# The last piece of w_down in fifteen loads of unequal rows

## The chip, the cores and the metric

The kernel runs on one core of one Trainium2 chip. The metric is the device time of one execution in microseconds. All numbers here are in float32, and all data come from HBM through one stream that the host has laid out in the order in which the kernel loads it.

## The reference

One decode step of two parallel branches, added to the input:

```python
B, Sq, D = 2, 1, 512;  Hq, Hkv, Sk, Dh = 32, 32, 8192, 128;  F = 1376
W = 2048                                   # the last 2048 cached positions
xn = layernorm(x)
q = (xn @ wq).reshape(B, Sq, Hq, Dh).transpose(0, 2, 1, 3)
scores = einsum("bhqd,bhkd->bhqk", q, k_cache[:, :, Sk - W:]) * Dh ** -0.5
o = einsum("bhqk,bhkd->bhqd", softmax(scores), v_cache[:, :, Sk - W:])
attention = o.transpose(0, 2, 1, 3).reshape(B, Sq, Hq * Dh) @ wo
ffn = ((xn @ w_gate) * (xn @ w_up)) @ w_down
return x + attention + ffn
```

Nearly all bytes are the two caches: 32 heads of 128 x 4096 numbers each, for keys and for values, where the 128 partitions hold 64 slices of the positions for each of the two batch entries.

## The kernel before

`loads()` is a hand-written list of loads in the order of their issue. Each entry is a step number, a buffer and the fields that the load brings: `k` and `v` are one head of a cache (4096 columns), `wq` a piece of the query projection, `wo` one head's 512 columns of the output projection, `wd` 128 rows of w_down (512 columns), `wg` and `wu` the gate weights. Three buffers of 13824 columns (`step0` to `step2`) are used in turn, and a small one (`extra`) holds the first fields and one late head of values.

`build()` first walks over the list, lays the fields side by side in their buffer and puts one load for each entry into `queue`: all 128 partitions, the columns of its fields, and the next stretch of the stream. `issue(upto)` then sends the queued loads up to a step to the queue of the engine SP. The last call, `issue(99)`, sends the loads of step 24: the values of head 31, then w_down pieces 1 to 4, 5 to 7, and 8 and 9. They go into buffer 0, over columns whose earlier contents have been used.

For each head of keys VectorE (DVE) multiplies the tile by the query and sums over the 128 numbers of a position (`products`, `sums`); for each group of four heads it forms the softmax weights (`weights`, with ScalarE's exponentials), and TensorE (PE) multiplies the weights with the values (`weigh`), gathers the parts (`fold`, `gather`, `scaled`) and applies the output projection (`wo`). PE also runs the feed-forward branch; `down(c, ...)` multiplies its hidden vector with w_down piece `c`. There are `NFC` = 10 such full pieces, numbered 0 to 9, and a rest of 96 rows that ScalarE's queue loads at the start (`wr`).

Most results add up in the PSUM bank `acc`. The last few go to another bank, `acc_g`, as `[128, 128]` blocks (`add_groups`: four matmuls for each piece). The end of `build()` is written out by hand:

```python
for i in range(5, 8):
    down(i, add_rows, (i - 5), last=True)
dve.tensor_tensor(acc_sb, acc, xr, op=ALU.add)
wo(d, add_groups)
for i in range(8, NFC):
    down(i, add_groups)
add_groups(id4, acc_sb, last=True)
dve.tensor_copy(o_out, acc_g)
pr.load("SP", out, o_out)
```

So `acc_sb`, on DVE, takes the sums of everything up to piece 7; PE meanwhile multiplies the last head, piece 8 and piece 9, then adds `acc_sb` by a matmul with a small selection matrix, DVE copies the block out of PSUM and SP stores it.

`Program` records every operation and works out the dependencies from the boxes that each one reads and writes. In `emit()` each load gets a semaphore of its own that is complete at 16; an operation that depends on several others gets a separate wait instruction for each but the last (line 196), which is attached to the operation itself (line 197). All operations are emitted from line 197, so groups are told apart here by their tiles.

Of the kernel before, what the change touches and what calls it, by code (L numbers as in the profile page):

```python
# [10 lines left out]
P = 128  # L11
# [8 lines left out]
NFC = F // P  # L20
# [8 lines left out]
CK, CO = J * DH, D  # L29
# [6 lines left out]
def loads():  # L36


    def units(kind, *ids):
        w = {"k": CK, "v": CK, "wo": CO, "wd": CO, "wq": HG * DH}[kind]  # L40
        return [(kind, i, w) for i in ids]

    def wq(g, *cs):
        return units("wq", *[(g, c) for c in cs])

    big = {
        1: units("k", 0, 1, 2),
        3: units("k", 3, 4) + units("v", 0),
        4: units("k", 5, 6) + units("v", 1),
        5: units("k", 7, 8) + units("v", 2),  # L50
    }
    k, v = 9, 3
    for n in range(6, 20):
        i = 1 + n % 2
        big[n] = units("k", *range(k, k + i)) + units("v", *range(v, v + 3 - i))
        k, v = k + i, v + 3 - i
    big[20] = units("k", 30, 31) + units("v", 24)
    big[21] = units("v", 25, 26, 27)
    big[22] = units("v", 28, 29)
    small = {  # L60
        1: wq(1, 0, 1, 2),
        3: wq(1, 3) + wq(2, 0, 1),
        4: wq(2, 2, 3) + units("wd", 0),
        5: wq(3, 0, 1, 2),
        6: units("wo", 0, 1, 2),
        7: wq(3, 3) + units("wo", 3) + wq(4, 0),
        8: units("wo", 4, 5, 6),
        9: units("wo", 7) + wq(4, 1, 2),
        10: wq(4, 3) + wq(5, 0, 1),
        11: units("wo", 8, 9, 10),  # L70
        12: units("wo", 11) + wq(5, 2, 3),
        13: wq(6, 0, 1, 2),
        14: units("wo", 12, 13, 14),
        15: units("wo", 15) + wq(6, 3) + wq(7, 0),
        16: units("wo", 16, 17, 18),
        17: units("wo", 19) + wq(7, 1, 2),
        18: wq(7, 3),
        19: units("wo", 20, 21, 22),
        20: units("wo", 23, 24, 25),
        21: units("wo", 26, 27),  # L80
        22: units("wo", 28, 29, 30, 31),
    }
    out = [
        (0, "x", [("c", 0, CX)] + wq(0, 0, 1, 2, 3)),
        (1, 0, big[1] + small[1]),
        (2, 1, [(w, 0, NC * F) for w in ("wg", "wu")]),
        (3, 2, big[3] + small[3]),
    ]
    for n in range(4, 23):
        out += [(n, (1, 0, 2)[(n - 4) % 3], big[n] + small[n])]  # L90
    out += [
        (23, "x", units("v", 30)),
        (24, 0, units("v", 31)),
        (24, 0, units("wd", 1, 2, 3, 4)),
        (24, 0, units("wd", 5, 6, 7)),
        (24, 0, units("wd", 8, 9)),
    ]
    return out


class Program:
# [133 lines left out]
def build(nc, stream, x_nat, wd_rest, out):  # L235
# [38 lines left out]
    got, used, queue, pos = {}, {}, [], 0  # L274
    for n, t, fields in loads():
        tile = buf_x if t == "x" else buf[t]
        c0 = used.get(n, 0)
        for kind, i, w in fields:
            c = used.get(n, 0)
            got[kind, i] = tile[:, c : c + w]  # L280
            used[n] = c + w
        c1 = used[n]
        assert c1 <= tile.shape[1], (n, c1)
        src = stream[pos : pos + P * (c1 - c0)].rearrange("(p i) -> p i", p=P)
        pos += P * (c1 - c0)
        queue.append((n, tile[:, c0:c1], src))
# [17 lines left out]
    c0 = got["c", 0]  # L304
# [193 lines left out]
    def has(n, kind):  # L498
        return [i for k, i, _ in plan.get(n, []) if k == kind]

    plan = {}
    for n, _, fields in loads():
        plan.setdefault(n, []).extend(fields)
# [19 lines left out]
    for n in range(3, 21):  # L523
        ks, vs = has(n, "k"), has(n, "v")
# [86 lines left out]
def laid_out(x):  # L611

    import numpy as np

    a = x["A_x"].reshape(B, D)
    xs = np.zeros((P, CX), a.dtype)
    xs[:, : B * NC] = a.reshape(B, P, NC).transpose(1, 0, 2).reshape(P, B * NC)
    o = B * NC
    for r in range(4):
        for n in range(N):  # L620
            xs[4 * n + r :: 32, o + r * N + n] = 1.0
    o += 4 * N
    for n in range(HG):
        for q in range(4):
            xs[32 * q + n, o + 4 * n + q] = 1.0
    o += 4 * HG
    for n in range(NFB):
        for b in range(B):
            xs[32 * n + b, o + n * B + b] = 1.0
    o += 2 * NFB  # L630
    for j in range(4):
        for b in range(B):
            xs[32 * j + b, o + b] = 1.0
    xs[:, o + 2 :] = a[:, 0]
    cache = {
        kind: x[name][:, :, SK - W :, :].reshape(B, H, HB, J * DH).transpose(1, 0, 2, 3)
        for kind, name in (("k", "A_k_cache"), ("v", "A_v_cache"))
    }
    wq = x["A_wq"].reshape(P, NC, H * DH)
    wo = x["A_wo"].reshape(H, P, D)  # L640
    gu = {
        kind: x[name].reshape(P, NC * F)
        for kind, name in (("wg", "B_w_gate"), ("wu", "B_w_up"))
    }
    wd = x["B_w_down"]

    def field(kind, i):
        if kind == "c":
            return xs
        if kind in ("k", "v"):  # L650
            return cache[kind][i].reshape(P, CK)
        if kind == "wq":
            g, c = i
            return wq[:, c, g * HG * DH : (g + 1) * HG * DH]
        if kind == "wo":
            return wo[i]
        if kind == "wd":
            return wd[i * P : (i + 1) * P]
        return gu[kind]

    parts = [
        np.concatenate([field(kind, i) for kind, i, _ in fields], axis=1).ravel()
        for _, _, fields in loads()
    ]
    return {"stream": np.concatenate(parts), "x": a, "wd_rest": wd[NFC * P :]}


# [25 lines left out]
```

## Time and profile before

| | |
|---|---|
| median of the runs (2) | 377.8 us (377.79 to 377.8) |
| the profiled execution | 377.87 us, of which the span is 376.5 us |
| granted TensorE clock | 0.719 of full speed on average |
| DVE | 302.9 us busy (80%), 166 instructions |
| PE matmuls | 194.0 us busy (52%), 844 instructions |
| loads on SP's queue | 4176 packets, 159.35 MB, 98.3% of the span on 16 DMA engines |
| HBM read | 159.49 MB, 424 GB/s over the span |

The span runs from the first to the last instruction. The share of a DMA queue is the time that its packets took on the sixteen DMA engines of the core, out of sixteen times the span. A packet is one row of a load or the small write that tells of its completion. PE's records come in two kinds, weight loads (PEld, LDWEIGHTS) and matmuls; a float32 matmul takes two of each. The letters "q" behind an engine's name (SPq, PEldq) stand for its sequencer: waits and the issuing of loads.

### The profile page before, as it was taken

The page shows a single profiled execution, that of the slowest core. Times are in us where ns is not written, and L with a number is a line of the kernel's source. Part 1 is how long each engine was busy: PE and PEld are TensorE (multiplying, and loading weights), DVE is VectorE, ACT ScalarE, POOL GpSimd, SP SyncE. Part 2 cuts the span into 40 slices and gives each one's busy share as a digit, 9 for nine tenths or more (in the row PEclk, how much of TensorE's full clock was granted, in tenths as well). Part 3 has the DMA queues.
Part 4 walks back from the last instruction along what each step waited for, and adds up shares of the span by engine and source line. Part 5 has one row for each costly group of instructions (what it writes and reads, how often), then busy time and mean ns, then how long its engine had stood idle before and what let it go on. Part 6 is the DMA issues. An engine that isn't in the chain of part 4 may idle for free.

```text
span 376.5 us, 1954 instructions
## 1 busy us (share of the span) xinstructions
PE 194.0 (52%) x844; PEld 57.2 (15%) x844; DVE 302.9 (80%) x166; ACT 15.1 (4%) x29; POOL 2.6 (1%) x9
## 2 busy tenths in 40 slices
PE   0651848523753256716436283661647334158777
PEld 0210122100210011201011020110111011012222
DVE  3059979999999987899599499969969997999301
ACT  1000100000000000000100000000000001000100
POOL 2000000000000000000000000000000000000000
PEclk9966857686685656679665756658587686566999
DMA  8999899998998989989999999999999999899995
GB/s 324 470 393 487 376 470 452 389 470 383 464 464 382 464 388 460 464 388 458 399 448 464 394 452 423 429 460 405 441 458 435 396 446 460 379 453 405 427 423 216
DMA packets 4299, 159.66 MB, mean 424 GB/s; under 512 B 482, under 2 KB 610, under 8 KB 964
## 3 DMA queue, kind: packets, MB, share of 16 engines
q1 hardware_dynamic: 4176, 159.35, 98.3%
q10 hardware_dynamic: 116, 0.20, 0.1%
q8 instruction: 6, 0.10, 0.1%
q14 instruction: 1, 0.01, 0.0%
HBM read 159.49 MB, written 0.07 MB: 424 GB/s over the span
## 4 chain that ended last, share of the span: by engine, by line
DVE 54%; DMA 40%; PE 4%; issue 1%; another core or an unknown queue 1%; SPq 0%; DVEq 0%
DMA step<-in_stream_dram 40%; DVE step L197 27%; DVE s L197 25%; PE acc L197 2%; PE q L197 1%; DVE both L197 1%; PE tr L197 1%; DVE nm L197 0%; PE gu L197 0%; DVE mt L197 0%; DVE acc_sb L197 0%; DVE h_sb L197 0%; DVE mtt L197 0%; DVE rec L197 0%
## 5 line engine op out<-in xcount | busy, mean ns | idle before, releaser
L197 DVE TENSOR_TENSOR step<-step,q 128x4096 f32<-128x4096 f32 x32 | 141.1, 4408 | 37.8 <-DMA step<-in_stream_dram 37.8
L197 DVE TENSOR_REDUCE s<-step 128x32 f32<-128x4096 f32 x32 | 141.3, 4417 | 0.8
L197 PE MATMUL o_ps<-step,p 128*32 128x512 f32 x496 | 95.4, 866 | 57.0 <-DMA step<-in_stream_dram 55.4
L197 PE MATMUL q<-step,xnb 128*128 128x512 f32 x56 | 40.8, 866 | 28.0 <-DVE step L197 20.5
L197 PE MATMUL acc<-step,oT 128*2 128x512 f32 x62 | 23.7, 893 | 43.9 <-DVE oT L197 27.8
L197 PEld LDWEIGHTS o_ps<-step,p 128*32 128x32 f32 x496 | 21.1, 147 | 113.1 <-DMA step<-in_stream_dram 62.2
L197 PEld LDWEIGHTS q<-step,xnb 128*128 128x128 f32 x56 | 13.5, 268 | 55.6 <-DVE step L197 25.7
L197 ACT ACTIVATE p<-s,zero 64x128 f32<-64x128 f32 x16 | 6.4, 399 | 264.5 <-DVE s L197 264.4
L197 DVE TENSOR_TENSOR oT<-gu,rec 128x8 f32<-128x8 f32 (+2 forms) x9 | 1.4, 158 | 18.5 <-PE gu L197 18.5
L197 PE MATMUL gu<-step,xn 128*2 128x512 f32 (+1 forms) x48 | 9.8, 733 | 7.7 <-DMA step<-in_stream_dram 7.7
L197 PE MATMUL tr<-both,ones 128*128 128x24 f32 (+1 forms) x18 | 4.3, 317 | 17.7 <-DVE both L197 17.6
L197 PE MATMUL gu<-cst,o_sb 128*128 128x8 f32 (+2 forms) x72 | 9.5, 258 | 3.0 <-ACT o_sb L197 2.8
L197 PEld LDWEIGHTS gu<-cst,o_sb 128*128 128x128 f32 x72 | 8.7, 191 | 12.3 <-ACT o_sb L197 10.2
L197 PEld LDWEIGHTS acc<-step,oT 128*2 128x2 f32 x62 | 1.6, 82 | 54.0 <-DVE oT L197 28.5
L197 PE MATMUL q<-xnb,s 128*32 128x512 f32 x8 | 5.9, 903 | 5.3 <-DVE s L197 5.3
L197 PEld LDWEIGHTS tr<-both,ones 128*128 128x128 f32 x18 | 3.3, 229 | 28.2 <-DVE both L197 28.2
L197 ACT COPY o_sb<-o_ps 128x512 f32<-128x512 f32 x9 | 5.3, 586 | 50.2 <-PE o_ps L197 50.2
L197 PE MATMUL q<-extra,xnb 128*128 128x512 f32 x8 | 5.8, 890 | 1.9 <-DVE xnb L197 1.9
L197 DVE TENSOR_REDUCE nm<-tr 64x4 f32<-64x8 f32 x16 | 2.6, 163 | 4.7 <-PE tr L197 4.6
L197 PEld LDWEIGHTS gu<-step,xn 128*2 128x2 f32 x48 | 2.2, 100 | 15.8 <-DMA step<-in_stream_dram 9.1
L197 PE MATMUL tr<-st,mean_w 128*128 128x4 f32 x2 | 0.6, 364 | 7.3 <-DVE st L197 7.3
L197 PE MATMUL gu<-cst,h_sb 128*128 128x6 f32 x8 | 1.9, 361 | 4.3 <-DVE h_sb L197 4.3
(54 smaller groups left out, 42.8 us busy)
## 6 DMA issues: line engine op xcount, KB each, us to landing
step<-in_stream_dram SPq DMA_DIRECT2D x18, 6912.0 KB, 31.2
step<-in_stream_dram SPq DMA_DIRECT2D x1, 6656.0 KB, 37.1
step<-in_stream_dram SPq DMA_DIRECT2D x1, 6400.0 KB, 30.1
step<-in_stream_dram SPq DMA_DIRECT2D x1, 5504.0 KB, 34.1
step<-in_stream_dram SPq DMA_DIRECT2D x1, 5120.0 KB, 26.2
extra<-in_stream_dram SPq DMA_DIRECT2D x1, 2048.0 KB, 30.7
step<-in_stream_dram SPq DMA_DIRECT2D x1, 2048.0 KB, 27.2
extra<-in_stream_dram SPq DMA_DIRECT2D x1, 1057.0 KB, 5.7
```

What stands on the lines that cost most here:

```text
L197: ins = getattr(e, method)(*args, **kw)
```

## The change

Pieces 8 and 9 of w_down no longer come in one load. Piece 8 gets a load of its own, and piece 9 comes in fifteen loads of 9, 15, 14, 13 and so on down to 2 rows, together 128. Each of these has rows of its own length: the first has 512 columns, and each further one 16 columns more, up to 736. The columns beyond 512 are zeros that the host puts into the stream; they land in unused columns to the right of the piece, and nothing reads them. The matmuls are the same; those of piece 9 now depend on fifteen loads.

```diff
@@ loads()
-        (24, 0, units("wd", 8, 9)),
+        (24, 0, units("wd", 8)),
+        (24, 0, units("wd", 9)),
     ]
     return out
+
+
+def parcels():
+    ks = [9] + list(range(15, 1, -1))
+    return [(k, CO + 16 * i) for i, k in enumerate(ks)]
@@ build(), filling the queue
         c1 = used[n]
         assert c1 <= tile.shape[1], (n, c1)
+        if fields[0][:2] == ("wd", NFC - 1):
+            lo = 0
+            for k, w in parcels():
+                src = stream[pos : pos + k * w].rearrange("(p i) -> p i", p=k)
+                pos += k * w
+                queue.append((n, tile[lo : lo + k, c0 : c0 + w], src))
+                lo += k
+            assert lo == P
+            continue
         src = stream[pos : pos + P * (c1 - c0)].rearrange("(p i) -> p i", p=P)
         pos += P * (c1 - c0)
         queue.append((n, tile[:, c0:c1], src))
@@ laid_out(), on the host
+    parts = []
+    for _, _, fields in loads():
+        f = np.concatenate([field(kind, i) for kind, i, _ in fields], axis=1)
+        if fields[0][:2] == ("wd", NFC - 1):
+            lo = 0
+            for k, w in parcels():
+                parts.append(np.pad(f[lo : lo + k], ((0, 0), (0, w - CO))).ravel())
+                lo += k
+        else:
+            parts.append(f.ravel())
```

More of the change, by code (lines that the diff above doesn't have):

```diff
@@ L659, in field @@
         return gu[kind]
[L661 to L664, printed above, removed]
+    parts = []
[8 more added lines that the diff above has]
+            parts.append(f.ravel())
     return {"stream": np.concatenate(parts), "x": a, "wd_rest": wd[NFC * P :]}
```

## The prediction

> **What bounds the kernel now.** I read the page first, then the chain that ended last over its final stretch, then the instructions of the last 5 us, then the DMA engines in short windows, then the waits of one source line.
>
> ```profile
> span 376.5 us, 1954 instructions
> q1 hardware_dynamic: 4176, 159.35, 98.3%
> q10 hardware_dynamic: 116, 0.20, 0.1%
> q8 instruction: 6, 0.10, 0.1%
> step<-in_stream_dram SPq DMA_DIRECT2D x18, 6912.0 KB, 31.2
> step<-in_stream_dram SPq DMA_DIRECT2D x1, 1024.0 KB, 20.9
> ```
>
> The loads fill 98.3% of sixteen DMA engines' time: the kernel is bound by its stream from HBM until just before the end. The last row is the load that changes, the 1024 KB of w_down pieces 8 and 9.
>
> What sets the end is in the chain, from 349 us on:
>
> ```profile
> 349.41 20.93 DMA step<-in_stream_dram
> 370.34 0.04 issue
> 370.38 1.04 PE acc L197 x8
> 371.42 0.98 PE gu L197 x8
> 372.40 0.54 PE acc L197 x3
> 373.43 0.70 DVE acc_sb L197
> 374.13 0.04 issue
> 374.17 0.45 PE q L197 x8
> 374.64 0.29 DVE o_out L197
> ```
>
> The chain does not pass through the last load. It leaves the DMAs at 370.34 with pieces 1 to 4 and goes on through PE, the addition on DVE (`acc_sb`) and the closing matmuls at 374.17. The last load stands beside it:
>
> ```profile
> 372.78 0.80 PE L197 MATMUL q<-step,oT 128*2 128x128 f32 x7
> 373.43 0.69 DVE L197 TENSOR_TENSOR acc_sb<-acc,xr 128x512 f32<-128x512 f32 x1 [0.83 <-PE acc L197]
> 373.46 0.33 PEld L197 LDWEIGHTS q<-step,hT 128*2 128x2 f32 x16 [0.17 <-DMA step<-in_stream_dram]
> 373.47 0.62 PE L197 MATMUL q<-step,hT 128*2 128x128 f32 x16
> 374.17 0.11 PEld L197 LDWEIGHTS q<-acc_sb,cst 128*2 128x2 f32 x8 [0.38 <-DVE acc_sb L197]
> 374.96 0.35 SPq L197 DMA_DIRECT2D out_dram<-o_out  x1
> ```
>
> The sixteen matmuls of pieces 8 and 9 start at 373.46, 0.04 us after the load lands (the same 0.04 stands in the chain at 370.34), and are issued by 373.79. Then PE stands 0.38 us until `acc_sb` is done. So even a last load that cost nothing would bring nothing: `acc_sb` holds the closing matmuls at 374.17. In the other direction the slack is 0.38 us.
>
> Why does the load land late? The DMA engines, by windows (the last two columns are the busy share of the sixteen and GB/s):
>
> ```profile
> 370.20:371.20 1.00, 0.82 (x8) 0.11 (x8) 0.00 (x0) 0.27 (x1) 0.00 (x0) 1.00 0.99 401
> 371.50:372.10 0.60, 0.60 (x7) 0.60 (x7) 0.00 (x0) 0.00 (x0) 0.00 (x0) 1.00 0.40 164
> 372.30:372.70 0.40, 0.40 (x5) 0.14 (x9) 0.16 (x1) 0.00 (x0) 0.00 (x0) 1.00 0.42 174
> 372.90:373.40 0.50, 0.50 (x14) 0.10 (x3) 0.00 (x0) 0.00 (x0) 0.00 (x0) 1.00 0.00 0
> ```
>
> Until 371.2 all sixteen work; from 371.5 only six or seven do, until 372.9. Nine are done about 1.45 us before the others. My reading: an instruction fetch takes one engine away from the stream for a while, and each of the six fetches of queue q8 (one row above) fell on another engine. Shares of about 0.4 are six or seven engines late by one fetch each.
>
> **The change, part by part.** The 1024 KB load becomes one of 512 KB (piece 8, 128 rows) and fifteen for piece 9: 9, 15, 14 and so on down to 2 rows, together 128, whose rows grow by 64 bytes a step from 2048 to 2944 bytes. The padding is 64 x (1x15 + 2x14 + ... + 14x2) = 42.6 KB; at the 401 GB/s above that is 0.11 us spread over all engines.
>
> *Issue on SP.* The three last loads are issued in one stretch, and the shortest load in the kernel has two rows:
>
> ```profile
> 349.41 1.28 SPq L197 DMA_DIRECT2D step<-in_stream_dram  x3
> 1.29 0.47 ACTq L197 DMA_DIRECT2D xr<-in_x_dram  x1
> ```
>
> That is 0.43 us each, and 0.47 for the load of two rows. Fifteen more take 6.5 to 7.1 us, so SP is done at about 358 instead of 350.7. Engines reach these rows at about 370.2 (1.25 us before 371.45), so 12 us of earlier loads hide it: nothing. Without that cover it would be 7 us. SP issues nothing else before the output.
>
> *Who moves the rows.* The q10 queue carried the loads `wr` (96 rows) and `xr` (2 rows): 98 row packets. Its 116 packets leave 18 completion packets; if `wr` leaves sixteen, as each q1 load does (29 x (128 + 16) = 4176), `xr` left two. So a load of two rows runs on two engines, and I take a load of k rows to run on k, one row each. If every load deals from the same first engine, the engines get 15, 15, 14, 13, 12, 11, 10, 9, 8, 6, 5, 4, 3, 2, 1 and 0 rows, where now each gets eight. If loads start at rotating engines, each gets about eight and nothing is skewed. I take the first. The Trainium skill says the same (DMA: Bandwidth & Descriptors, "Why a DMA increments its semaphore by 16 and not by 1": largest count up to 16 that divides the rows, on the lowest-numbered engines).
>
> One engine moves 401/16 = 25 GB/s. Now: 8 x 4096 bytes = 1.31 us. After, for the first engine: piece 8, 8 x 2048 bytes, 0.65; then fifteen rows of 2496 bytes on average, 0.100 each, plus 0.01 for each completion packet (not shown by a row; between 0 and the 0.03 of 768 bytes), 1.65. Together 2.30, or +1.0 us. Likewise the fourth engine (13 rows) is at about +0.75, the ninth (8 rows) at +0.1, the last at -0.65. Break-even is at seven rows.
>
> So it hangs on which engines are late. A punctual one can carry +1.0, since it has 1.45 in hand. If one of the first two is among the six late ones, the landing moves from 373.42 to 374.4; if the late ones are the high-numbered, the landing does not move or comes earlier. The trace does not number the engines. By chance, neither of the first two is late with 10/16 x 9/15 = 0.38, so more likely one is.
>
> *Waits on PE.* The matmuls of piece 9 now wait for fifteen semaphores instead of one: fourteen wait instructions of their own and one on the first weight load. Queued behind them on PE: the eight matmuls of piece 9, the closing eight, then the copy and the output. The price of one, from the rows of the line that emits waits:
>
> ```profile
> L196 SPq EVENT_SEMAPHORE  x10: 17/17/17, 72.4 to 303.9; - x10
> L196 PEldq EVENT_SEMAPHORE  x1: 51/51/51, 52.2 to 52.2; - x1
> ```
>
> Fourteen at 51 ns are 0.71 us; at the 17 ns of SP's 0.24. I take 51, PE's own. They run after piece 8's matmuls are issued. Piece 8 lands by about 372.8, so PE reaches it straight after the `q<-step,oT` matmuls, is through by about 373.5, and leaves the waits at 374.2 if all have landed. Eight matmuls of piece 9 take half of the 0.33 us, so the closing ones start at 374.4 instead of 374.17: +0.2. Where the first engines are late, the waits for earlier pieces pass during the wait for the last, and only the landing counts: 374.4 + 0.04 + 0.2 = 374.64, +0.45. The two do not add. The bounds of this part are thus 0 (waits that cost nothing, late engines high-numbered) and +0.45.
>
> *Sum.* Padding 0.0 to 0.1 (inside the landing), issue 0, skew or waits +0.45, against the profiled execution's own 377.87 (its span 376.5 and 1.37 around it): 378.3. The two runs' median is 377.8, 0.07 below the profiled one, so I forecast 378.3 after rounding 378.25.
>
> **The rivals.**
> *A. Neighbouring rows get in each other's way.* Now an engine's eight rows lie far from most others'; afterwards each small load puts rows of adjacent partitions on up to fifteen engines at once. If four neighbouring partitions share one way in, a row takes up to four times as long: eleven loads of 4, two of 3, two of 2 row times, 54 x 0.1 = 5.4 us instead of 1.5 for the first engines. For: nothing in this trace has such small loads; against: `xr`'s rows in partitions 0 and 1 are too few to tell. The full price lands at 370.2 + 0.65 + 5.4 + 0.5 = 376.75, +2.8. Engines that fall apart in time overlap less, so I take a third to a half of that: +0.9 to +1.4, 378.7 to 379.2, say 379.0. It decides as soon as the punctual engines lose their 0.45 us of remaining reserve. The Trainium skill speaks for it (SBUF — State Buffer, "Door 1: The DMA port swizzle"): groups of four partitions share a port, and sixteen partitions reached 104 GB/s there.
>
> *B. Not slower.* The late engines are all high-numbered, or the skew fits them, and PE's sequencer hides the waits: `acc_sb` at 374.13 still decides, 377.8. For: the 0.38 us of slack; against: 0.71 us of waits on PE behind a start at 373.5.
>
> *C. The change does not do what it says.* Loads rotate over the engines, rows are even, landing as now plus 0.1; the waits then give +0.2: 378.0.
>
> *D. SP is late.* If a load of an odd number of rows costs SP not 0.45 but over (370.2 - 350.7)/15 = 1.3 us, the rows come after their engines are ready; at 2 us each SP ends at 380.7 and the kernel at about 387. For: no load here has an odd number of rows; against: the two rows of `xr` took 0.47.
>
> **How the numbers follow.** Forecast (first engines late, or waits: +0.2 to +0.6) 0.45; A 0.30; B 0.12; C 0.08; D 0.03; other 0.02. The range 377.6 to 379.6 takes in all but the upper part of A and D. Two per cent, about what a measurement of this kernel can tell from no change, is 7.5 us: only D reaches it on the slow side, nothing in the profile on the fast side. So within 2% 0.95, slower 0.04, faster 0.01; in sign I expect a small loss.
>
> **What would show it.** Right: fifteen loads issued by about 358, each 0.4 to 0.5 us; the row of the closing matmuls at about 374.6; the chain now ending through the last load or the waits, not `acc_sb`; fourteen wait rows on PE near 374; DMA share falling in steps until 373 to 374. Wrong: a DMA tail beyond 374.5 with rows of 2 to 3 KB each taking several times 0.1 us (A); closing matmuls still at 374.17 after `acc_sb` (B); an even tail (C); SP issuing beyond 370 (D).

## The result, and the profile after

The changed kernel takes 380.09 us (median of two runs, 379.97 and 380.2) against 377.8. The ratio is 1.0059 [1.0043, 1.0075]: no difference by the 2% bound, but slower by 2.3 us and outside the predicted 377.6 to 379.6. The profiled execution took 379.97 us, 378.6 of it in the span and 1.37 around it as before, so the loss lies inside the span.

The page after, its span, its queue and three of its DMA issues (KB of a load, median us from issue to landing; a load lands when its semaphore is complete); the last row is one of the fifteen small loads:

```profile
span 378.6 us, 1976 instructions
q1 hardware_dynamic: 4432, 159.40, 97.9%
...
step<-in_stream_dram SPq DMA_DIRECT2D x1, 768.0 KB, 23.1
step<-in_stream_dram SPq DMA_DIRECT2D x1, 256.0 KB, 23.4
step<-in_stream_dram SPq DMA_DIRECT2D x1, 30.9 KB, 22.6
```

The same row of the kernel before, for the load of pieces 5 to 7:

```profile
step<-in_stream_dram SPq DMA_DIRECT2D x1, 768.0 KB, 22.4
```

The queue carried 256 packets more. Piece 8 alone leaves 128 rows and 16 completions, so piece 9 left 256: 128 rows and 128 completions, one for each row. Fifteen loads with sixteen completions each would have left 368. So a load of k rows runs on k engines, and each of them also writes a completion. Pieces 5 to 7, issued ahead of everything that changed, land 0.7 us later than before.

The chain that ended last (start, duration, what):

```profile
354.57 0.04 issue
354.61 20.96 DMA step<-in_stream_dram
375.57 0.45 issue
376.02 0.66 PE q L203 x16
376.68 0.02 issue
376.71 0.29 DVE o_out L203
```

It now goes through the last loads, as predicted, and no longer through `acc_sb`. The load issued at 354.61 is the one of six rows. It lands at 375.57, where before the last landing was 373.42, and PE starts 0.45 us behind it instead of 0.04. The DMA engines in the windows shown for before, and in two more (the last two columns are the busy share of the sixteen and GB/s):

```profile
370.20:371.20 1.00, 0.81 (x8) 0.11 (x8) 0.00 (x0) 0.30 (x1) 0.00 (x0) 1.00 1.00 365
371.50:372.10 0.60, 0.60 (x7) 0.60 (x7) 0.00 (x0) 0.00 (x0) 0.00 (x0) 1.00 0.60 158
372.30:372.70 0.40, 0.12 (x2) 0.03 (x1) 0.16 (x1) 0.00 (x0) 0.00 (x0) 1.00 0.66 148
372.90:373.40 0.50, 0.45 (x8) 0.15 (x11) 0.00 (x0) 0.00 (x0) 0.00 (x0) 1.00 0.40 140
373.80:374.30 0.50, 0.50 (x17) 0.30 (x11) 0.26 (x1) 0.00 (x0) 0.00 (x0) 1.00 0.00 0
374.30:375.00 0.70, 0.12 (x5) 0.00 (x0) 0.43 (x1) 0.00 (x0) 0.00 (x0) 1.00 0.00 0
```

Two things stand here. From 371.5 the engines are busier than before (0.60 against 0.40, then 0.66 against 0.42) and yet move fewer bytes (158 against 164 GB/s, 148 against 174): rows take longer. And from 373.8 on nothing moves at all, though the last load lands only at 375.57. The tail is 1.7 us in which all packets have run and the landings are still to come. By the trace's records of the packets, the completions' own among them, the last one ends at 373.84, and a completion packet takes 0.01 us. In the kernel before, the last packet of the load ended at 372.95 and the load landed 0.47 us later.

The end by instructions (start, duration, engine and operation; in brackets the idle time before it):

```profile
373.93 0.49 PE L203 MATMUL q<-step,hT 128*2 128x128 f32 x7
374.04 0.69 DVE L203 TENSOR_TENSOR acc_sb<-acc,xr 128x512 f32<-128x512 f32 x1 [1.42 <-PE acc L203]
375.99 0.14 PEld L203 LDWEIGHTS q<-step,hT 128*2 128x2 f32 x8 [1.87 <-issue]
376.02 0.40 PE L203 MATMUL q<-step,hT 128*2 128x128 f32 x8 [1.60 <-DMA step<-in_stream_dram]
376.13 0.21 PEld L203 LDWEIGHTS q<-acc_sb,cst 128*2 128x2 f32 x8
377.02 0.38 SPq L203 DMA_DIRECT2D out_dram<-o_out  x1
```

`acc_sb` is ready at 374.73 and waits for piece 9. The closing matmuls start at 376.13 instead of 374.17 and the store at 377.02 instead of 374.96: +2.06, nearly all of the 2.1 us by which the span grew.

### The profile page after: what moved, and what is told of

Its sections match the earlier page's. It is cut to its first block, busy times and chain, and to the rows that moved or that the text cites. A ratio compares the mean times of both kernels' runs of the same rounds, so it can differ in the third digit from the quotient of the medians.

```text
span 378.6 us, 1976 instructions
## 1 busy us (share of the span) xinstructions
PE 189.0 (50%) x844; PEld 55.3 (15%) x844; DVE 303.0 (80%) x166; ACT 15.1 (4%) x29; POOL 2.6 (1%) x9
## 4 chain that ended last, share of the span: by engine, by line
DVE 49%; DMA 47%; PE 2%; SPq 1%; issue 1%
DMA step<-in_stream_dram 47%; DVE s L203 24%; DVE step L203 23%; SPq L203 1%; DVE both L203 1%; PE acc L203 1%; PE tr L203 1%; DVE mt L203 0%; DVE nm L203 0%; DVE mtt L203 0%; DVE mc L203 0%; PE q L203 0%; DVE rec L203 0%; DVE oT L203 0%; DVE o_out L203 0%
## 5 line engine op out<-in xcount | busy, mean ns | idle before, releaser
L203 PE MATMUL q<-step,xnb 128*128 128x512 f32 x56 | 36.7, 787 | 27.9 <-DVE step L203 19.8
L203 PEld LDWEIGHTS q<-step,xnb 128*128 128x128 f32 x56 | 12.6, 251 | 54.2 <-DVE step L203 24.9
```

Of the source, the lines that this page charges most:

```text
L203: ins = getattr(e, method)(*args, **kw)
```

## The experiments

The theory after this profile: the completions of one engine arrive at the semaphores one after another, about 0.2 us apart, however short the rows between them are (from the trace's records of the semaphores: successive landings lie 0.18 to 0.21 us apart). So every load has a fixed price on each engine that takes part in it. The records do not number the engines; an engine is known here by the even steps of its landings. The rival: rows are slow because neighbouring partitions are written at once (rival A of the prediction), or because they lie side by side in HBM. Beside them stand the price of the waits on PE and the question whether a lighter last load could win anything. The median of the kernel before on these chips was 377.92 to 377.95. Unless said otherwise the diffs are against the changed kernel. They are cut: where loads are written as first row, step, rows and columns, the lines that work out the dependencies and lay out the stream change with them and are not shown.

**Eight loads of 16 neighbouring rows (e1_near16)** take the staircase away: every engine gets eight rows of 2048 bytes and nine loads in all, piece 8 included.

```diff
-    ks = [9] + list(range(15, 1, -1))
-    return [(k, CO + 16 * i) for i, k in enumerate(ks)]
+    return [(16 * i, 1, 16, CO) for i in range(8)]
```

> Piece 9 comes in eight loads of 16 neighbouring rows of 2048 bytes: every engine moves one row of each load, eight in all, so nothing is skewed. Completion theory (each load costs every engine that it uses about 0.19 us, one after the other, however short its row): last landing about 0.65 + 8 x 0.19 us after pieces 5 to 7, which the late engines finish at 372.2 when undisturbed: 374.4, closing matmuls at about 374.7, device time +0.5 us against the kernel before (378.3). Neighbour theory (rows of adjacent partitions slow each other): pieces 5 to 7 land late too, at 372.6 to 372.9, row packets of 2048 bytes take two to four times the 0.084 us that they take alone, and the time is +0.8 us or more. Skew theory (only which engine has more rows counts): as before, 377.8 to 378.0.

379.0 us, ratio 1.0034 [1.0021, 1.0047]. Its chain:

```profile
354.02 20.93 DMA step<-in_stream_dram
374.95 0.04 issue
375.00 0.66 PE q L210 x16
```

The last landing is at 374.95, +1.53 over before, with as many bytes on each engine as before. By the trace's records piece 8 lands at 373.32, and the eight loads follow 0.20 to 0.22 apart. So the skew is not needed for most of the loss.

**The same, with the rows of a load eight partitions apart (e2_far16).**

```diff
+    return [(i, 8, 16, CO) for i in range(8)]
```

> The same eight loads of 16 rows, but each load's rows lie eight partitions apart, so that neighbours never move together. Completion theory: still 8 x 0.19 us behind piece 8, +0.5 us against the kernel before, whatever the partitions. Neighbour theory: row packets back to nearly 0.084 us, pieces 5 to 7 land at 372.2 as before, and the time falls to that of the kernel before plus at most 0.2 us. If both hold, it lies below the contiguous one by what the earlier pieces lost, about 0.3 to 0.7 us.

378.91 us, ratio 1.0027 [1.0016, 1.0037].

```profile
355.05 19.92 DMA step<-in_stream_dram
374.97 0.04 issue
```

374.97 against 374.95. It does not matter how near the rows of one load lie to each other: rival A, as it was stated, falls. The 0.3 to 0.7 us that the neighbour theory would have given back did not come.

**The staircase with rows eight partitions apart (e3_far_stair).** Loads of 8, 15, 14 down to 1 rows, sixteen of them, rows widening as in the change; most lines that choose the row numbers are left out.

```diff
+    ks = [8] + list(range(15, 0, -1))
...
+            out.append((cls, 8, k, CO + 16 * i))
```

> The staircase with rows eight partitions apart: sixteen loads of 8, 15, 14 and so on to 1 rows, of the same lengths as in the changed kernel (one load more, and the sixth engine has eleven rows instead of ten). Completion theory: pieces 5 to 7 land at 372.2 to 372.4 again, then 0.7 us for piece 8 and 11 x 0.19 us on the late sixth engine: last landing about 375.1, time about 379.5, only 0.5 us below the changed kernel. Neighbour theory: the rows take 0.1 us each again, last landing 373.8 to 374.2, time about 378.3.

380.14 us, ratio 1.0059 [1.0044, 1.0074]; the last landing is at 375.72 against 375.57. Neighbours make no difference to the staircase either. (The expectation gives the sixth engine one row more than in the change. That is a slip: eleven loads have six rows or more in both, which fits the two landings.)

**All fifteen loads on one semaphore (e4_one_sem)**, so that PE waits once, for 240.

```diff
-            w = [(sem[key], 16 if ops[j][5] else at[j]) for key, j in waits[i]]
...
+                if j == self.shared[0]:
+                    w.append((sem[key], 16 * len(self.shared)))
```

> The changed kernel, but the fifteen loads count on one semaphore, so PE waits once for all of them and not fifteen times. If the waits of PE that follow the last landing cost what the changed kernel shows (0.42 us from the landing at 375.57 to the weight load at 375.99), the last landing stays at 375.5 and the time falls by about 0.4 us to 379.7. If the waits are covered, nothing changes: 380.1.

379.47 us, ratio 1.0041 [1.0026, 1.0056].

```profile
355.96 19.71 DMA step<-in_stream_dram
375.66 0.04 issue
375.71 0.66 PE q L215 x16
```

The landing stays (375.66), the gap behind it falls from 0.45 to 0.04. So the waits cost 0.4 us behind the landing; in the medians it is 0.6, with intervals that overlap. One semaphore instead of fifteen leaves the landing where it was, so the 0.2 us do not come from changing semaphores.

**Tiny rows (e5_tiny).** The kernel before, with the last 128 columns of piece 9 in eight loads of 16 rows of 512 bytes: the same bytes, and no engine gets more than before. Against before (`small` is 128 for the last load and 0 for the others):

```diff
+        c1 -= small
...
+        for lo in range(0, P if small else 0, 16):
+            src = stream[pos : pos + 16 * small].rearrange("(p i) -> p i", p=16)
+            pos += 16 * small
+            queue.append((n, tile[lo : lo + 16, c1 : c1 + small], src))
```

> The kernel before (pieces 8 and 9 in one load of 128 rows), but the last 128 columns of piece 9 come in eight further loads of 16 rows of 512 bytes; the bytes in all are the same. This leaves almost only the number of loads. Completion theory: the big load lands at about 373.3, then every engine has eight more completions of about 0.2 us each although a 512-byte row takes 0.03 us: last landing 374.9, time +1.0 us against the kernel before (378.9), as with eight loads of 2048-byte rows. Theory that the rows themselves are slow: 8 x 0.03 us after 373.3, last landing 373.5, time 377.9.

378.97 us, ratio 1.0027 [1.0015, 1.0038]. Its DMA issues, then its chain:

```profile
step<-in_stream_dram SPq DMA_DIRECT2D x1, 768.0 KB, 22.5
step<-in_stream_dram SPq DMA_DIRECT2D x1, 448.0 KB, 23.2
step<-in_stream_dram SPq DMA_DIRECT2D x8, 8.0 KB, 21.9
```

```profile
354.12 20.94 DMA step<-in_stream_dram
375.06 0.04 issue
375.10 0.61 PE q L198 x10
```

Pieces 5 to 7 land as before (22.5), the bytes are the same, and still the last landing comes 1.64 us later than before. By the trace's records the 448 KB load lands at 373.56 and the eight small ones follow to 375.06, 0.19 each, although one of their rows took 0.027 us and a completion packet 0.009. This shows that the price hangs on the load and not on its bytes.

**Four loads of 32 rows (e6_rows32).**

```diff
+    return [(32 * i, 1, 32, CO) for i in range(4)]
```

> Piece 9 in four loads of 32 rows, two rows for each engine, instead of eight loads of 16 rows. Completion theory: half the completions, 4 x 0.2 us behind piece 8, which is about the 4 x 2 x 0.08 us that the rows take anyway: last landing 374.0 to 374.2, time 378.0 to 378.2. If small loads slow everything down in proportion to their bytes, as with eight loads: 378.9.

378.56 us, ratio 1.0018 [1.0009, 1.0027]; the profiled execution was the shortest of ten, 378.2.

```profile
352.09 22.05 DMA step<-in_stream_dram
374.15 0.04 issue
```

Piece 8 lands at 373.39 by the trace's records, and four loads follow to 374.15, 0.19 each. Each engine moves two rows of 0.084 us in each of these loads, so the step is not rows plus 0.2 us: the rows lie inside it. The landing is where it was expected, the median (378.0 to 378.2 expected) 0.4 us above.

**HBM rows 8192 bytes (`PITCH`, 2048 numbers) apart (e7_far_src)**, otherwise the eight loads of 16 neighbouring rows:

```diff
-                src = stream[pos : pos + k * w].rearrange("(p i) -> p i", p=k)
-                pos += k * w
+                src = stream[pos : pos + k * PITCH].rearrange("(p i) -> p i", p=k)[:, 0:w]
+                pos += k * PITCH
```

> The eight loads of 16 neighbouring rows, but in HBM each row begins 8192 bytes after the one before instead of 2048, so that engines do not read neighbouring rows at the same moment. This asks what slows the late engines' rows of pieces 5 to 7 (6144 bytes in up to 0.40 us instead of 0.24) and makes them land at 372.7 instead of 372.2. If reading neighbouring rows of HBM does it: 372.2 again, last landing 374.4, time 378.4. If the completions do it, or the writing side: 372.7, last landing 374.95 and 378.9 to 379.0 as with rows close together. The 8 x 0.2 us of completions stay in either case.

378.97 us, ratio 1.0028 [1.0018, 1.0037]; landing at 374.79, and pieces 5 to 7 as late as ever, 23.1 us after their issue. It is not the side-by-side rows in HBM that slow the others.

**The staircase with rows of 4096 bytes (e8_wide).**

```diff
-    return [(k, CO + 16 * i) for i, k in enumerate(ks)]
+    return [(k, 2 * CO) for i, k in enumerate(ks)]
```

> The changed kernel's fifteen loads with all rows 1024 columns (4096 bytes; the second half zeros that nothing reads), 524 KB for piece 9 instead of 305 KB. Completion theory: a row of 4096 bytes takes 0.16 us, still less than a completion, so the last landing stays at 375.6 to 375.9 and the time at 380.1 to 380.4. If the bytes of the rows set the pace, each row on the late engines takes half as long again or more, ten of them: last landing 376.4 or later, time 381 or more.

380.72 us, ratio 1.0074 [1.0059, 1.0089].

```profile
step<-in_stream_dram SPq DMA_DIRECT2D x1, 768.0 KB, 23.8
step<-in_stream_dram SPq DMA_DIRECT2D x1, 256.0 KB, 24.6
```

Bytes do count, by a second way: wider small rows make pieces 5 to 7 and piece 8 land 0.7 and 1.2 us later than in the change. By the trace's records it is the late engines that land them last; they are still at these rows while the punctual ones write piece 9. The last landing, 376.42, is 0.85 behind that of the change, where the expectation from completions alone was 375.6 to 375.9. On the engine that ends last the landings follow 0.30 to 0.39 us apart over the first loads, where rows of 4096 bytes took up to 0.45 us, and 0.17 to 0.20 over the last eight (such a row takes 0.16 us unhindered).

**Eight loads of 128 rows and 64 columns (e9_cols).** As many loads as in e1_near16, but each has all 128 rows, dealt out over the engines as in every large load, so that each engine keeps to the partitions that it writes there. Against before, with piece 8 in a load of its own:

```diff
+        step = 64 if fields[0][:2] == ("wd", NFC - 1) else c1 - c0
+        for c in range(c0, c1, step):
...
+            queue.append((n, tile[:, c : c + step], src))
```

> Piece 9 again in eight loads, but each brings 64 columns of all 128 partitions (rows of 256 bytes), so every engine writes the same partitions as in the large loads; bytes and number of loads are as with eight loads of 16 rows. The completions stay: 8 x 0.2 us behind piece 8. What is asked is why pieces 5 to 7 land at 372.6 to 372.9 instead of 372.2 (22.9 to 23.1 us after their issue instead of 22.4). If a group of partitions takes in only about one engine's stream, so that a punctual engine's rows in a late engine's partitions cost the late one time: 22.4 us again, last landing 374.5, time 378.5. If it is small loads as such: 22.9 us, last landing 374.95, time 378.95.

378.37 us, ratio 1.0013 [1.0004, 1.0022]. Its DMA issues, then two instructions of its end:

```profile
step<-in_stream_dram SPq DMA_DIRECT2D x1, 768.0 KB, 22.5
step<-in_stream_dram SPq DMA_DIRECT2D x1, 256.0 KB, 22.6
step<-in_stream_dram SPq DMA_DIRECT2D x8, 32.0 KB, 20.0
```

```profile
374.13 0.09 PEld L198 LDWEIGHTS q<-step,hT 128*2 128x2 f32 x2 [0.28 <-DMA step<-in_stream_dram]
374.54 0.09 PEld L198 LDWEIGHTS q<-step,hT 128*2 128x2 f32 x2 [0.32 <-DMA step<-in_stream_dram]
```

Pieces 5 to 7 are punctual again (22.5): the slowing of the late engines is gone. This run alone does not say why, since its rows are also short, and e5_tiny with its rows of 512 bytes had no slowing either. The completions stay, and can be read on PE: a block of 128 columns needs two of these loads, and two blocks start 0.41 us apart, 0.205 for a load. The landing at 374.49 and the time are as expected.

**Pieces 8 and 9 in one load each (e10_split).** Against before:

```diff
-        (24, 0, units("wd", 8, 9)),
+        (24, 0, units("wd", 8)),
+        (24, 0, units("wd", 9)),
```

> One half of the change alone: pieces 8 and 9 in a load each, both of 128 rows. One completion more on each engine, hidden in 0.65 us of rows: last landing 373.4 to 373.5, the closing matmuls still held by acc_sb at 374.17, time 377.8 to 378.0 in either theory.

377.98 us, ratio 1.0001 [0.9992, 1.001].

```profile
373.54 0.70 DVE acc_sb L198
374.25 0.04 issue
374.29 0.44 PE q L198 x8
```

`acc_sb` still decides. Pieces 8 and 9 land at 372.97 and 373.60 by the trace's records, the latter 0.18 later than before, inside the slack of 0.38: the part of the change that splits the two pieces costs nothing. The two landings lie 0.63 us apart, the time of eight rows of 2048 bytes: where an engine's rows take longer than 0.2 us, the completion is hidden. Pieces 5 to 7 are not slowed, although the punctual engines move rows of the same 2048 bytes beside them as in e6_rows32: a row of 6144 bytes took at most 0.25 us here and up to 0.41 there (trace's records).

**The closing order alone (e11_order)**: `acc_sb` after pieces 1 to 4, pieces 5 to 7 straight into the last bank, and pieces 8 and 9 last of all. Against before:

```diff
     for i in range(1, 5):
-        down(i, add_rows, i % 4, last=(i == 4 - 1))
+        down(i, add_rows, i % 4, last=True)
+    dve.tensor_tensor(acc_sb, acc, xr, op=ALU.add)
...
     for i in range(5, 8):
-        down(i, add_rows, (i - 5), last=True)
-    dve.tensor_tensor(acc_sb, acc, xr, op=ALU.add)
+        down(i, add_groups)
     wo(d, add_groups)
+    add_groups(id4, acc_sb)
     for i in range(8, NFC):
-        down(i, add_groups)
-    add_groups(id4, acc_sb, last=True)
+        down(i, add_groups, last=(i == NFC - 1))
```

> The loads of the kernel before; the closing order on PE and DVE changed: acc_sb is formed right after pieces 1 to 4, pieces 5 to 7 go to the last bank, and acc_sb is added ahead of pieces 8 and 9. If acc_sb holds the closing matmuls in the kernel before, as its chain shows, the last landing at 373.4 now sets the end: the copy out of PSUM starts at 374.1 instead of 374.64 and the time is 0.5 us lower, 377.3. If the end hangs on something else, 377.8.

377.48 us (377.28 to 379.0), ratio 0.9993 [0.9984, 1.0001].

```profile
371.49 0.69 DVE L197 TENSOR_TENSOR acc_sb<-acc,xr 128x512 f32<-128x512 f32 x1 [4.54 <-PE acc L197]
373.47 0.62 PE L197 MATMUL q<-step,hT 128*2 128x128 f32 x16
374.16 0.29 DVE L197 COPY o_out<-q 128x128 f32<-128x128 f32 x1 [1.56 <-PE q L197]
```

The copy comes at 374.16 instead of 374.64, and the span is 376.1 instead of 376.5. That `acc_sb` held the end of the kernel before is shown; the device time is not clearly shorter, since the interval reaches 1.0001.

**Order and split together (e12_order_split)**, the most that these runs suggested:

> The new closing order, with pieces 8 and 9 in a load each. PE then has only eight matmuls behind the last landing instead of sixteen: another 0.15 us lower than with one load, 377.15, if one more completion costs nothing behind 0.65 us of rows; the same as with one load or above, if it does cost its 0.2 us.

378.35 us (377.2 to 379.03), ratio 1.0003 [0.9993, 1.0013], inconclusive. The span of the profiled execution was 376.0, its copy at 374.05, and yet the execution took 378.69: 2.7 us outside the span, where the others have 1.3 to 1.4. In e11_order it was 2.0 us. In these two traces alone a further 16 KB instruction load on queue q8 runs behind the end of the span (at 377.29 and 377.72); these kernels have 1990 and 1991 instructions, the kernel before 1954. Whether that load is what lengthens them is not shown. No version that beats the kernel before was found beyond doubt.

## Why the prediction was wrong

**Right.** SP is done with its issues at 357.0 (predicted 358):

```profile
349.44 7.58 SPq L203 DMA_DIRECT2D step<-in_stream_dram  x18
```

So D fell. The sign (a small loss), the engines that move the rows and the path through the last load were right. A load of k rows runs on k engines, and the landing is decided by a late engine that is low enough in the order to take part in many loads: here the sixth, in the load of six rows, and in e8_wide the fourth, in the load of four (issued at 355.33 there, landed at 376.42). The chain leaves `acc_sb` for the last load, and a lighter last load had nothing to win (e10_split). By the trace's records the late engines were not the same ones in every profile, so their place is chance, as the prediction assumed. Its reading of why they are late also comes out of the trace of before: the number of engines whose completions come 0.8 us or more behind the middle one rises by one with each of the six fetches on q8 (each 16 KB in 1.02 to 1.10 us). A seventh became late with an 8 KB packet on q14 at 90.3, which the prediction did not count.

**The step that failed is the price of a load on an engine**: the prediction added the time of the row and "0.01 for each completion packet (not shown by a row; between 0 and the 0.03 of 768 bytes)", and took the landing to come when that sum is done. The packet does take 0.01 us. What the runs showed in its place is that the landings of one engine follow each other no closer than about 0.2 us, and that the rows run on meanwhile. A load costs an engine the longer of the two, its rows or 0.2 us. By the trace's records of the landings:

| kernel | the load ahead lands | small loads after it | last landing | per load |
|---|---|---|---|---|
| e6_rows32 | 373.39 | 4 | 374.15 | 0.19 |
| e9_cols | 372.99 | 8 | 374.49 | 0.19 |
| e7_far_src | 373.45 | 8 | 374.79 | 0.17 |
| e1_near16 | 373.32 | 8 | 374.95 | 0.20 |
| e5_tiny | 373.56 | 8 | 375.06 | 0.19 |
| the change | 373.56 (the first, of 9 rows) | 10 on the sixth engine | 375.57 | 0.20 |

The trace of before could not show the cost, since the landings of an engine lay 1.2 us apart there, with eight rows of 4096 bytes between them. So an unknown cost was bounded by the time of its packet, and that was the wrong measure. By the prediction's own prices the sixth engine, with eleven rows, is done after 0.65 + 11 x 0.105 = 1.8 us, against 1.31 in the kernel before: +0.5. With 0.2 us for each of the eleven loads it is 2.85, or +1.54. The first engines, which the prediction took to be the slowest, matter only if they are late: every engine's time is set by how many loads it takes part in.

The Trainium skill (DMA: Bandwidth & Descriptors, "Anatomy of one DMA") gives, for a DMA that GpSimd issues, about 2 us of fixed cost, most of it the receipt of its last write, and calls the semaphore write itself essentially free. The loads here are issued by SP, and no run shows the fixed cost of one alone: the store of the output, which has no load ahead of it, landed 1.5 us after its issue in the kernel before. The second half agrees with the 0.01 us of a completion packet. For completions that follow each other on one engine the measured 0.2 us decides.

**The second mis-sized term** is the rows themselves, which the prediction took at the stream's 25 GB/s. Small loads with rows of 2048 bytes or more slow the late engines: pieces 5 to 7 land 0.7 us later, 1.4 with 4096-byte rows (23.8 against 22.4). They are not slowed by rows of 512 bytes (e5_tiny), nor by loads of 128 rows, of 256 bytes (e9_cols) or of 2048 (e10_split). So neither the number of loads nor the length of the rows does it alone. What is left is which engine writes which partition: that a row in a partition which another engine is filling slows that engine. This is argued, not shown. If a large load gave each engine eight neighbouring rows, e2_far16 too would keep each engine to its own partitions; if it dealt the rows out in turn, e1_near16 would. Both were slowed, so the argument needs a third way of dealing, and no trace here shows which rows an engine gets. Rival A foresaw such crowding and gave 379.0, nearer than the forecast, but by luck: its place was wrong. It is not within a small load (e2_far16 equals e1_near16), and there a row was not slow enough to count: one of 2496 bytes took 0.10 to 0.18 us in the change (trace's records), less than the 0.2 from landing to landing. The price, 0.3 to 0.7 us at piece 8 (373.32 in e1_near16, 373.65 in the change), lies on the loads ahead of the small ones. The Trainium skill (SBUF — State Buffer, "Door 1: The DMA port swizzle") has groups of partitions share a port; e10_split against e6_rows32 is compatible with a shared way in, but no run here tells ports from other causes.

**The third: "The two do not add."** They do. The argument was that earlier waits pass during the wait for the last landing. But PE's waits do not stand in the order of the landings: the load of six rows was the last to land, and other waits stood behind the one for it. The rows of the line that emits waits:

```profile
L202 PEldq EVENT_SEMAPHORE  x8: 51/51/51, 52.2 to 375.9; - x8
```

Seven of these instructions are new, not fourteen, since each takes two semaphores. Four of the seven pass after the landing at 375.57, from 375.60 to 375.91 and 0.1 us apart: the one for the load of six rows, and three for loads that were already there. e4_one_sem prices what stands behind the landing at 0.4 us.

**The sum as measured.** Unhindered, piece 8 lands at 372.97 to 372.99 (e10_split, e9_cols), and in the kernel before the rows of piece 9 took the last landing to 373.42, 0.44 further. In the change piece 8 lands at 373.65 (+0.67, slowed rows), and the completions end 1.92 behind it instead of 0.44 (+1.48, against the +1.54 worked out above): 2.15 in all. The split between the two is rough, since piece 8 lands last on another engine than the sixth, whose first small load, of 9 rows, landed at 373.56 already. Then the waits, 0.38 (375.57 to 375.99, less the 0.04 that was there); less the slack of 0.38; less 0.19, since eight matmuls stand behind the landing instead of sixteen (0.14 against 0.33 us of weight loads). That is +1.96 at the closing matmuls, 376.13, where +0.45 was predicted. Who is late and through whom the chain runs was right. The price of a load on an engine was half of what it is, the slowing of the loads ahead was missing, and the waits were left out of the sum.

## What to carry to other kernels

Near the end of a stream, count loads and not only bytes: each load takes each engine that takes part in it about 0.2 us from landing to landing, however small its rows are, and more only if its rows there take longer. Keep the last loads few, over all 128 partitions, and what must be waited for at the end on one semaphore; one split was free here only because the other operand of the sum came later anyway. Before making the last load lighter, look in the chain whether the end hangs on it at all: here it hung on `acc_sb`.

## What the runs showed of the hardware

- Completions of one engine arrive 0.17 to 0.22 us apart, whether the rows between them have 256 bytes (eight an engine, e9_cols), 512 (e5_tiny) or 4096 (the last loads of e8_wide), though their packets take 0.01 us. Where the rows take longer, the rows set the step (0.63 us in e10_split).
- A load whose completions do not queue landed 0.47 us (before) and 0.43 us (e10_split) after its last packet.
- Loads of 32 rows or fewer, with rows of 2048 bytes or more, slow the rows that other engines are still moving. In the trace's records a row of 6144 bytes took up to 0.41 us on a late engine in the change, and up to 0.25 before, in e9_cols and in e10_split. Why is open.
- An instruction fetch makes one DMA engine late, and it stays late: the six on q8 left six engines about 1.4 to 1.6 us behind the others at the end of the stream, and the 8 KB packet on q14 a seventh, 0.9 us behind (trace of before).
- Issuing can stall. Eleven loads took SP 20.0 us in e9_cols, where eight of them have 128 rows of 256 bytes, and 6.3 us in e2_far16 with eight loads of 16 rows:

```profile
349.51 20.02 SPq L198 DMA_DIRECT2D step<-in_stream_dram  x11
```

```profile
349.34 6.30 SPq L210 DMA_DIRECT2D step<-in_stream_dram  x11
```

  Single issues took up to 11 us there. It cost nothing that the end shows, since the last was issued by 369.5. Why is not shown; many rows outstanding is a guess.
- A load of 16 rows with a step between its partitions costs SP 0.56 to 0.60 us (e2_far16) instead of 0.42 to 0.43 (e1_near16).
